# First x chunk loaded as two wide transfers, V two tiles ahead, first numerator products inside the dense tail, and another order in the last tile

## The chip, the cores and the metric

The kernel runs on one core of a Trainium2 chip. The metric is device time in microseconds (us) of that core, lower is better, given as the median of several runs. One execution was also taken with the hardware profiler: that execution has its own time, and the span inside it, from the first to the last recorded instruction, is what all the rows of the profile are measured on.

## What is computed

Two branches read the same `x` of 2048 tokens with 512 features, and a gate per token mixes them. Branch A is linear attention with 32 heads of 16 features, with a feature map made of two softmaxes; branch B is a dense layer with relu between two matrices (512 to 1376 to 512). All inputs are bf16.

```python
g = sigmoid((x * gate_w).sum(-1, keepdims=True))
# A
qkv = (x @ wqkv) split into q, k, v of 32 heads x 16
pq, pk = q @ w_phi[h], k @ w_phi[h]              # 16x16 per head
phi_q = concat([softmax(pq), softmax(-pq)], -1)  # 32 features per head
phi_k = concat([softmax(pk), softmax(-pk)], -1)
kv = einsum("bhsf,bhsd->bhfd", phi_k, v);  z = einsum("bhsf->bhf", phi_k)
num = einsum("bhqf,bhfd->bhqd", phi_q, kv)
den = einsum("bhqf,bhf->bhq", phi_q, z)[..., None] + 1e-6
a = (num / den) reshaped to (2048, 512) @ wo
# B
b = maximum(x @ w1, 0) @ w2
out = g * a + (1 - g) * b
```

The sums `kv` and `z` run over all tokens, so no output of branch A can be finished before all tokens have passed the feature map; the order of the tokens does not matter to them.

## The kernel before, in words

**Tiles.** The 2048 tokens are 16 tiles of 128 (m = 0 to 15) and four chunks of 512 (c = 0 to 3). `XT` holds x transposed, features on partitions. `PS` is the matmul memory with 8 banks of 512 f32 columns. `HT` holds the hidden layer of branch B, 11 blocks of 128 rows (kt = 0 to 10, the last with 96).

**How the order is made.** A small planner (`_Plan`, lines 14 to 55) collects instructions per engine in the order in which the program calls them, each with the names of the events that it waits for; every engine then works through its own list strictly in that order. So the order of the calls at lines 452 to 495 is the order of each engine, of the transfers that an engine issues too. The engines are TensorE (PE), VectorE (DVE), ScalarE (ACT), GpSimd (POOL) and SyncE (SP, which issues most transfers).

**Start (lines 143 to 208).** SP issues four loads of x, tokens j*128 to j*128+127 into `XS[:, j, :]` (line 145; `XS` is the first part of the tile `OT`, which is free until the end of the kernel), then four tiny loads of the gate weights into an extra column of W1. POOL issues the loads of W1 in three parts, of WV and of w_phi. Seven dummy matmuls run on PE (`warm`, line 178). Then PE transposes the first chunk of x, tile by tile, with an identity (line 186), and DVE and ACT in turn copy the four results into `XT`. SP meanwhile waits for the last part of W1 and for WV (line 163), and then issues the transposing load of Wq and Wk (`wqk`, line 164), and those of x chunks 1 to 3 (line 166). POOL waits for the last of these before it loads W2 and WO (lines 168 to 173).

**Pieces of work.**
- `hunit(c, kt)` (line 216): 4 matmuls of 512 columns for one block of the hidden layer, in banks 3, 4, 5 in turn; unit number u uses bank 3 + u % 3. ACT does the relu into `HT` (line 242). For kt = 10 the extra column gives the gate's logits: ACT copies that row (`GROW`, line 234) and issues a small transfer that lays it out by tokens in `GL` (line 238).
- `pre(half)` (line 246): Wq (half 0) or Wk (half 1) times the block-diagonal w_phi, 16 matmuls of 128 columns in banks 0, 1, 6, 7, copied out by DVE and ACT in turn (lines 263, 266). It needs `wqk`. The first of them also waits for event `cv1`, the copy of V tile 1.
- `vtile(m)` (line 315): V of a tile, 4 matmuls into bank 2 (tile 1: bank 0), copied to `VS` by DVE for the first four tiles and by ACT for the others (lines 328, 330). `VS` and `FM` have NB = 5 buffers.
- `atile(m)` (line 269): pq and pk of a tile, 8 matmuls into banks 0 and 1; then ACT takes two exponentials of 1024 columns each, of + and of - the banks (line 287). The next tile's matmuls wait for the second exponential, since they write the same banks. DVE sums and inverts (lines 290 to 299), POOL scales (lines 302 to 308), SP issues a transposing transfer of the q features to `PHQ` (line 311, event `tq`).
- `kv(m)` (line 333): 8 small matmuls that add the tile to kv and z in banks 6 and 7. `kvfin()` (line 346): four DVE instructions that mask kv and z into `KVNZ`, the last with event `kvz1`.
- `gate()` (line 360): one exponential on ACT over `GL`, and three small DVE instructions.
- `nd(m)` (line 368): numerator and denominator of a tile, 8 matmuls of 68 columns, banks 0, 1 for even m and 2, 3 for odd m; DVE inverts and multiplies (lines 380, 384, event `om`), SP issues a transposing transfer into `OT` (line 389, event `to`).
- `finB(m)` (line 392): 11 matmuls with W2 into bank 5 or 4. `finA(m)` (line 403): 4 matmuls with WO into bank 6 or 7, once `to` of the tile has landed; ACT scales by the gate (`TFA`, line 413, event `ta`). `comb(m)` (line 417): DVE adds the two halves (event `cb`), SP stores.
- `last(m)` (line 426): for tile 15 `finB` in two halves of 256 columns, with `finA` between them, and two combines and two stores.

**The order before.** 11 units of chunk 0; V tiles 0 and 1; `pre(0)`; V tile 2; `pre(1)`; V tile 3. Then for each m: `atile(m)`, `vtile(m)` from m = 4 on, one or two units of chunks 1 and 2 (22 in all: two for each of the first four tiles and in tiles 9 and 15, one otherwise), and `kv(m - 3)`. Then the 11 units of chunk 3, with the last three `kv` between them (before units 0, 2 and 6, counted from 0). Then `kvfin`, `gate`, `finB(0)`, `nd(0)`, `nd(1)`, `finB(1)`, `nd(2)`, `finA(0)`, `comb(0)`, `finA(1)`, `comb(1)`, and for m = 2 to 14 `nd(m + 1)`, `finB(m)`, `finA(m)`, `comb(m)`; then `last(15)`.

`nd(1)` and `finB(0)`, `finB(1)` wait for the relu of the very last unit (`rl{hcount[0] - 1}`).

Of the kernel before, what the change touches and what calls it, by code (L numbers as in the profile page):

```python
# [57 lines left out]
def bass_gated_mix__linear_kernel_hedgehog__dense_activation_relu__prompt_kernel(  # L58
# [31 lines left out]
    with ExitStack() as es:  # L90
# [52 lines left out]
        p.op("dve", lambda e: e.memset(WARM[:, :], 1.0), ev="warm")  # L143
        for j in range(4):
            p.dma("sp", lambda e, j=j: e.dma_start(out=XS[:, j, :], in_=x2[j * P:(j + 1) * P, :]),
                  f"x0{j}", ev=f"x0{j}")
        load_w1(0)
# [35 lines left out]
        for j in range(4):  # L183
            tp = PS[:, XB[j], :].bitcast(BF16)[:, 0:512]
            for dt in range(NDT):
                p.op("pe", lambda e, tp=tp, j=j, dt=dt: e.transpose(
                    tp[:, dt * P:(dt + 1) * P], XS[:, j, dt * P:(dt + 1) * P], IDN[:, :]),
                    after=["idn", f"x0{j}"], ev=(f"xt{j}" if dt == NDT - 1 else None))
            src = tp.rearrange("p (a b) -> p a b", a=NDT)
            dst = XT[:, :, j * P:(j + 1) * P]  # L190
            if j % 2 == 0:
                p.op("dve", lambda e, s=src, d=dst: e.tensor_copy(d, s), after=[f"xt{j}"], ev=f"xc{j}")
            else:
                p.op("act", lambda e, s=src, d=dst: e.activation(d, s, ACT.Copy), after=[f"xt{j}"], ev=f"xc{j}")
# [51 lines left out]
        def pre(half):  # L246
            PB = [0, 1, 6, 7]
            for i in range(4 * half, 4 * half + 4):
# [3 lines left out]
                after = ["wqk"] + [f"wbd{g}" for g in range(NDT)]  # L252
                if i == 0:
                    after.append("cv1")
                if i >= 4:
# [59 lines left out]
        def vtile(m):  # L315
            b = m % NB
            bank = 0 if m == 1 else 2
            prev = {0: [], 1: [], 2: ["cv0"]}.get(m, [f"cv{m - 1}"])
            for dt in range(NDT):
                p.op("pe", lambda e, m=m, dt=dt, bank=bank: e.matmul(  # L320
                    PS[:, bank, :], XT[:, dt, m * P:(m + 1) * P], WV[:, dt, :],
                    start=(dt == 0), stop=(dt == NDT - 1)),
                    after=((xready(m // 4) + ["wv"] + prev) if dt == 0 else ()),
                    ev=(f"v{m}" if dt == NDT - 1 else None))
            dst, src = VS[:, b, :, 0:64], PS[:, bank, :].rearrange("p (g c) -> p g c", g=NG)
            after = [f"v{m}"] + ([f"kv{m - NB}"] if m >= NB else [])
            if m < 4:
                p.op("dve", lambda e, d=dst, s=src: e.tensor_copy(d, s), after=after, ev=f"cv{m}")  # L328
            else:
                p.op("act", lambda e, d=dst, s=src: e.activation(d, s, ACT.Copy), after=after, ev=f"cv{m}")  # L330
# [29 lines left out]
        def gate():  # L360
# [5 lines left out]
                 after=["g"], ev="gt")  # L366

        def nd(m):
            b0 = 2 * (m % 2)
            after = [f"tq{m}", "kvz1"] + ([f"om{m - 2}"] if m >= 2 else [f"em{NT - 1}", f"cv{NT - 1}"])  # L370
            if m == 1:
                after.append(f"rl{hcount[0] - 1}")
            for g in range(NG):
# [18 lines left out]
        def finB(m):  # L392
            bank = 5 - m % 2
            after = ["w2"]
            after += [f"cb{m - 2}"] if m >= 2 else [f"rl{hcount[0] - 1}"]
            for kt in range(KT):
# [20 lines left out]
        def comb(m):  # L417
# [5 lines left out]
            p.dma("sp", lambda e, m=m, ob=ob: e.dma_start(  # L423
                out=o2[m * P:(m + 1) * P, :], in_=OSB[:, ob, :]), f"out{ob}", after=[f"cb{m}"], ev=f"out{m}")

        def last(m):
            ob = m % 3
            for hf in range(2):
                if hf == 1:
                    finA(m)  # L430
                bank = (5 - m % 2, 0)[hf]
                cs = slice(hf * 256, hf * 256 + 256)
# [7 lines left out]
            for hf in range(2):  # L440
                bank = (5 - m % 2, 0)[hf]
                cs = slice(hf * 256, hf * 256 + 256)
# [9 lines left out]
        for kt in range(KT):  # L452
            hunit(0, kt)
        vtile(0)
        vtile(1)
        pre(0)
        vtile(2)
        pre(1)
        vtile(3)
        mid = [(c, kt) for c in (1, 2) for kt in [KT - 1] + list(range(KT - 1))]  # L460
        late = [(3, kt) for kt in [KT - 1] + list(range(KT - 1))]
        done = 0
        for m in range(NT):
            atile(m)
            if m >= 4:
                vtile(m)
            want = 2 * (m + 1) if m < 4 else 8 + (m - 3) * (len(mid) - 8) // (NT - 4)
            while done < want:
                hunit(*mid[done])
                done += 1  # L470
            if m >= LAG:
                kv(m - LAG)
        cuts = {0: NT - 3, 2: NT - 2, 6: NT - 1}
        for i, u in enumerate(late):
            if i in cuts:
                kv(cuts[i])
            hunit(*u)
        kvfin()
        gate()
        finB(0)  # L480
        nd(0)
        nd(1)
        finB(1)
        nd(2)
        finA(0)
        comb(0)
        finA(1)
        comb(1)
        for m in range(2, NT - 1):
            nd(m + 1)  # L490
            finB(m)
# [57 lines left out]
```

## Time and profile before

| | |
|---|---|
| median of 3 runs | 163.28 us (163.04 to 163.32) |
| profiled execution, its own time | 162.36 us |
| span of the profiled execution | 160.1 us |
| PE / DVE / ACT / POOL busy | 149.4 / 89.0 / 78.7 / 58.2 us |
| instructions | 2385 |

By stages of the span, PE's busy time:

| stage, us from the start of the span | length | PE busy |
|---|---|---|
| until the first hidden unit, 0 to 7.25 | 7.25 | 4.37 |
| hidden units of chunk 0, to 16.90 | 9.65 | 9.65 |
| first V tiles and `pre`, to 23.40 | 6.50 | 5.48 |
| loop over 16 tiles, to 88.10 | 64.70 | 62.78 |
| hidden units of chunk 3, to 98.40 | 10.30 | 10.29 |
| first output tiles, to 111.98 | 13.58 | 11.66 |
| steady output tiles, to 150.20 | 38.22 | 38.22 |
| last tiles, to 160.10 | 9.90 | 6.93 |

How to read it: an engine's busy time counts the recorded duration of its instructions. Matmuls of 512 columns are recorded with 0.38 us each, but they overlap: back to back, four of them take 0.87 us, so one occupies PE for 0.22 us. The chain of waits follows the work back from the last instruction to what released each step. A transfer's "us to landing" counts from the start of its issue.

### The profile page before, as it was taken

The numbers are of one execution on the slowest core, as the hardware profiler recorded it, in microseconds if no ns is written. First come the engines' busy times: TensorE is split into PE (matmuls) and PEld (weight loads), VectorE is DVE, ScalarE is ACT, GpSimd is POOL, SyncE is SP. The second block draws the span as 40 slices with busy tenths as digits, with TensorE's granted clock in tenths as the row PEclk, the third lists the DMA queues.
The fourth block names the chain that finished last, engine by engine and source line by source line (L and its number), as shares of the span: only waits on it lengthen the run. The fifth ranks groups of instructions, "written<-read, shape, count | busy, mean of one in ns | idle before, by whom it ended". The sixth has DMA issues, their size and how long they took to land.

```text
span 160.1 us, 2385 instructions
## 1 busy us (share of the span) xinstructions
PE 149.4 (93%) x930; PEld 72.6 (45%) x930; DVE 89.0 (56%) x145; ACT 78.7 (49%) x116; POOL 58.2 (36%) x63
## 2 busy tenths in 40 slices
PE   6699799899999999999999998979999999999983
PEld 2444354334444444444444543534444444544442
DVE  1401391788888878687888521544455544445532
ACT  3266456877777787777777665022211111221111
POOL 7400005678888887868788800000000000000000
PEclk9999999999999999999999999999999999999999
DMA  5868994952232232332225320043222232243222
GB/s 126 259 234 186 242 185 87 359 150 66 66 70 66 66 70 66 70 68 66 66 66 70 66 66 0 0 98 92 74 68 66 70 98 66 72 92 70 66 67 64
DMA packets 41242, 15.57 MB, mean 97 GB/s; under 512 B 37584, under 2 KB 40320, under 8 KB 41232
## 3 DMA queue, kind: packets, MB, share of 16 engines
q1 hardware_dynamic: 39568, 11.54, 32.8%
q0 software_dynamic: 1088, 3.88, 7.3%
q8 instruction: 7, 0.11, 0.3%
q10 hardware_dynamic: 576, 0.01, 0.2%
q14 instruction: 3, 0.02, 0.1%
HBM read 4.41 MB, written 2.10 MB: 41 GB/s over the span
## 4 chain that ended last, share of the span: by engine, by line
PE 66%; ACT 20%; DVE 5%; DMA 3%; issue 3%; ACTq 1%; DVEq 0%
PE PS L398 19%; ACT FM L287 17%; PE PS L278 17%; PE PS L228 14%; PE PS L408 8%; DMA OT<-OTM 3%; PE PS L320 3%; PE PS L178 2%; PE PS L374 2%; ACT TFA L413 1%; DVE VS L328 1%; DVE OTM L384 1%; PE PS L340 1%; DVE WkP L263 1%; ACT GROW L234 1%
## 5 line engine op out<-in xcount | busy, mean ns | idle before, releaser
L228 PE MATMUL PS<-XT,W 128*128 128x512 bf16 (+1 forms) x176 | 41.3, 379 | 0.7 <-DVE VS L202 0.7
L398 PE MATMUL PS<-W,HT 128*128 128x512 bf16 (+1 forms) x165 | 38.1, 379 | 0.9 <-ACT EG L361 0.8
L287 ACT ACTIVATE FM<-PS 128x1024 bf16<-128x1024 f32 x32 | 31.0, 1020 | 15.7 <-PE PS L278 15.7
L302 POOL TENSOR_TENSOR FM<-FM,SC 128x1024 bf16<-128x1024 bf16 x16 | 30.9, 1929 | 12.3 <-DVE SC L293 12.3
L413 ACT ACTIVATE TFA<-PS,GT 128x512 bf16<-128x512 f32 x16 | 11.0, 687 | 46.9 <-PE PS L408 46.9
L242 ACT ACTIVATE HT<-PS 128x512 bf16<-128x512 f32 (+1 forms) x44 | 25.6, 604 | 8.1 <-PE PS L228 5.8
L290 DVE TENSOR_REDUCE ZB<-FM 128x64 f32<-128x1024 bf16 x16 | 19.5, 1220 | 14.2 <-ACT FM L287 14.2
L228 PEld LDWEIGHTS PS<-XT,W 128*128 128x128 bf16 (+1 forms) x176 | 17.3, 100 | 20.5 <-DVE VS L202 0.9
L278 PE MATMUL PS<-WqP,XT 128*128 128x512 bf16 x64 | 24.4, 381 | 2.1 <-ACT FM L287 1.3
L419 DVE SCALAR_TENSOR_TENSOR OSB<-PS,OMG,TFA 128x512 bf16<-128x512 f32 x15 | 11.3, 751 | 25.2 <-ACT TFA L413 25.2
L278 PE MATMUL PS<-WkP,XT 128*128 128x512 bf16 x64 | 24.3, 379 | 0.0
L398 PEld LDWEIGHTS PS<-W,HT 128*128 128x128 bf16 (+1 forms) x165 | 15.1, 97 | 17.4 <-issue 1.2
L295 DVE TENSOR_REDUCE ZB<-FM 128x64 f32<-128x1024 bf16 x16 | 18.6, 1161 | 0.0
L408 PE MATMUL PS<-WO,OT 128*128 128x512 bf16 x64 | 16.4, 378 | 1.5 <-DMA OT<-OTM 1.5
L308 POOL TENSOR_TENSOR FM<-FM,SC 128x512 bf16<-128x512 bf16 x16 | 16.9, 1058 | 1.3
L320 PE MATMUL PS<-WV,XT 128*128 128x512 bf16 x64 | 16.3, 379 | 0.0
L384 DVE TENSOR_TENSOR OTM<-PS,RDEN 128x512 bf16<-128x512 f32 x16 | 11.1, 691 | 0.5
L278 PEld LDWEIGHTS PS<-WqP,XT 128*128 128x128 bf16 x64 | 6.2, 97 | 11.0 <-ACT FM L287 4.5
L408 PEld LDWEIGHTS PS<-WO,OT 128*128 128x128 bf16 x64 | 5.9, 97 | 9.3 <-DMA OT<-OTM 1.7
L320 PEld LDWEIGHTS PS<-WV,XT 128*128 128x128 bf16 x64 | 6.1, 98 | 7.1
L293 DVE RECIPROCAL SC<-ZB 128x64 f32<-128x64 f32 x16 | 8.8, 553 | 0.5
L278 PEld LDWEIGHTS PS<-WkP,XT 128*128 128x128 bf16 x64 | 6.3, 98 | 5.7
(53 smaller groups left out, 89.4 us busy)
## 6 DMA issues: line engine op xcount, KB each, us to landing
out_dram<-OSB SPq DMA_DIRECT2D x15, 128.0 KB, 1.7
W<-in_B_w_dram POOLq DMA_DIRECT2D x1, 1280.0 KB, 6.6
OT<-in_A_x_dram SPq DMA_DIRECT2D x4, 128.0 KB, 2.2
W<-in_B_w_dram POOLq DMA_DIRECT2D x1, 512.0 KB, 6.2
WV<-in_A_wqkv_dram POOLq DMA_DIRECT2D x1, 512.0 KB, 7.2
WO<-in_A_wo_dram POOLq DMA_DIRECT2D x1, 512.0 KB, 6.9
W<-in_B_w_dram POOLq DMA_DIRECT2D x1, 480.0 KB, 6.7
W<-in_B_w_dram POOLq DMA_DIRECT2D x1, 384.0 KB, 4.6
```

Source lines behind the costliest of these rows:

```text
L228: p.op("pe", lambda e, c=c, kt=kt, M=M, dt=dt, bank=bank: e.matmul(PS[0:M, bank, :], W1[:, dt, kt * P:kt * P + M], XT[:, dt, c * 512:(c + ...
L242: p.op("act", lambda e, c=c, kt=kt, Mr=Mr, bank=bank: e.activation(HT[0:Mr, kt, c * 512:(c + 1) * 512], PS[0:Mr, bank, :], ACT.Relu), afte ...
L278: p.op("pe", lambda e, m=m, dt=dt, which=which, W=W: e.matmul(PS[:, which, :], XT[:, dt, m * P:(m + 1) * P], W[:, dt, :], start=(dt == 0), ...
L287: p.op("act", lambda e, o=fm5[:, :, :, s, :], i=src, s=s: e.activation(o, i, ACT.Exp, scale=(1.0 if s == 0 else -1.0)), after=[f"qk{m}"] + ...
L290: p.op("dve", lambda e, b=b: e.tensor_reduce(ZB[:, b, 64:128], FM[:, b, 1, :].rearrange("p (g f) -> p g f", f=DH), AX.X, ALU.add), after=[ ...
L295: p.op("dve", lambda e, b=b: e.tensor_reduce(ZB[:, b, 0:64], FM[:, b, 0, :].rearrange("p (g f) -> p g f", f=DH), AX.X, ALU.add), after=([f ...
L302: p.op("pool", lambda e, b=b, fk=fk: e.tensor_tensor(fk, fk, SC[:, b, 64:128].unsqueeze(2).to_broadcast([P, 2 * H, DH]), ALU.mult), after= ...
L308: p.op("pool", lambda e, b=b, fq=fq: e.tensor_tensor(fq, fq, SC[:, b, 0:32].unsqueeze(2).to_broadcast([P, H, DH]), ALU.mult), after=[f"sc{ ...
L320: p.op("pe", lambda e, m=m, dt=dt, bank=bank: e.matmul(PS[:, bank, :], XT[:, dt, m * P:(m + 1) * P], WV[:, dt, :], start=(dt == 0), stop=( ...
L384: p.op("dve", lambda e, b0=b0, r=r, ob=ob: e.tensor_tensor(OTM[:, ob, :].rearrange("p (g h d) -> p g h d", g=NG, h=HG), bass.AP(tensor=PS, ...
L398: p.op("pe", lambda e, kt=kt, M=M, m=m, bank=bank: e.matmul(PS[:, bank, :], HT[0:M, kt, m * P:(m + 1) * P], W2[0:M, kt, :], start=(kt == 0 ...
L408: p.op("pe", lambda e, t=t, m=m, bank=bank: e.matmul(PS[:, bank, :], OT[:, t, m * P:(m + 1) * P], WO[:, t, :], start=(t == 0), stop=(t == ...
```

## The change

Four things are changed; the work that is computed stays the same.

- The first 512 tokens are laid out in another way: tile j of chunk 0 now holds the tokens 4p + j for p = 0 to 127. Two loads, each of two neighbouring tokens per partition (2 KB in a row), replace the four loads. The stores of tiles 0 to 3 go to the same tokens (`orow`). The transposes of tile j wait for load j // 2.
- V runs two tiles ahead: only V tiles 0 and 1 come before the loop, behind `pre(0)` and `pre(1)` in place of ahead of them, and the loop calls `vtile(m + 2)`. All V tiles use bank 2, and ACT copies from tile 2 on. `pre(0)` no longer waits for `cv1`. Inside the loop `kv(m - 3)` comes right behind `atile(m)`, then V, then the units, which are spread otherwise: two in tiles 3, 6, 10, 13, 14 and 15, one in the others.
- In the dense tail (the 11 units of chunk 3) `kvfin` now follows `kv(15)` ahead of unit 6, `gate` stands behind unit 5, `nd(0)` ahead of unit 8 and `nd(1)` behind unit 10. `nd(0)` and all odd tiles use banks 0 and 1, the even tiles from 2 on banks 2 and 3. `nd` now runs two tiles ahead of `finB` and `finA`. The waits for the last relu become waits for the last relu of the unit's own bank (`hlast`).
- The last tile runs `finA(15)` first, then both halves of `finB`; the second half uses bank 2.

```diff
-        for j in range(4):
-            p.dma("sp", lambda e, j=j: e.dma_start(out=XS[:, j, :], in_=x2[j * P:(j + 1) * P, :]),
-                  f"x0{j}", ev=f"x0{j}")
+        xq = x2[0:512, :].rearrange("(p j) d -> p j d", j=4)
+        oq = o2[0:512, :].rearrange("(p j) d -> p j d", j=4)
+        def orow(m):
+            return oq[:, m, :] if m < 4 else o2[m * P:(m + 1) * P, :]
+        for i in range(2):
+            p.dma("sp", lambda e, i=i: e.dma_start(out=XS[:, 2 * i:2 * i + 2, :], in_=xq[:, 2 * i:2 * i + 2, :]),
+                  f"x0{i}", ev=f"x0{i}")
...
-                    after=["idn", f"x0{j}"], ev=(f"xt{j}" if dt == NDT - 1 else None))
+                    after=["idn", f"x0{j // 2}"], ev=(f"xt{j}" if dt == NDT - 1 else None))
...
-                if i == 0:
-                    after.append("cv1")
...
-            bank = 0 if m == 1 else 2
-            prev = {0: [], 1: [], 2: ["cv0"]}.get(m, [f"cv{m - 1}"])
+            bank = 2
+            prev = [f"cv{m - 1}"] if m else []
...
-            if m < 4:
+            if m < 2:
...
+        def hlast(bank):
+            return f"rl{[u for u in range(hcount[0]) if 3 + u % NH == bank][-1]}"
         def nd(m):
-            b0 = 2 * (m % 2)
-            after = [f"tq{m}", "kvz1"] + ([f"om{m - 2}"] if m >= 2 else [f"em{NT - 1}", f"cv{NT - 1}"])
-            if m == 1:
-                after.append(f"rl{hcount[0] - 1}")
+            b0 = 0 if m == 0 or m % 2 else 2
+            after = [f"tq{m}", "kvz1"]
+            if m == 0:
+                after.append(f"em{NT - 1}")
+            elif m == 2:
+                after += [f"cv{NT - 1}", hlast(3)]
+            else:
+                after.append(f"om{max(m - 2, 0)}")
...
-            after += [f"cb{m - 2}"] if m >= 2 else [f"rl{hcount[0] - 1}"]
+            after += [f"cb{m - 2}"] if m >= 2 else [hlast(bank)]
...
-                out=o2[m * P:(m + 1) * P, :], in_=OSB[:, ob, :]), f"out{ob}", after=[f"cb{m}"], ev=f"out{m}")
+                out=orow(m), in_=OSB[:, ob, :]), f"out{ob}", after=[f"cb{m}"], ev=f"out{m}")
...
+            finA(m)
             for hf in range(2):
-                if hf == 1:
-                    finA(m)
-                bank = (5 - m % 2, 0)[hf]
+                bank = (5 - m % 2, 2)[hf]
...
+        pre(0)
         vtile(0)
+        pre(1)
         vtile(1)
-        pre(0)
-        vtile(2)
-        pre(1)
-        vtile(3)
...
             atile(m)
-            if m >= 4:
-                vtile(m)
-            want = 2 * (m + 1) if m < 4 else 8 + (m - 3) * (len(mid) - 8) // (NT - 4)
-            while done < want:
+            if m >= LAG:
+                kv(m - LAG)
+            if m + 2 < NT:
+                vtile(m + 2)
+            while done < (min(m + 1, 14) * (len(mid) - 4)) // 14 + 2 * max(m - 13, 0):
                 hunit(*mid[done])
                 done += 1
-            if m >= LAG:
-                kv(m - LAG)
-        cuts = {0: NT - 3, 2: NT - 2, 6: NT - 1}
         for i, u in enumerate(late):
-            if i in cuts:
-                kv(cuts[i])
+            if i == 0:
+                kv(NT - 3)
+            if i == 2:
+                kv(NT - 2)
+            if i == 6:
+                kv(NT - 1)
+                kvfin()
+            if i == 8:
+                nd(0)
             hunit(*u)
-        kvfin()
-        gate()
+            if i == 10:
+                nd(1)
+            if i == 5:
+                gate()
         finB(0)
-        nd(0)
-        nd(1)
-        finB(1)
         nd(2)
         finA(0)
         comb(0)
-        finA(1)
-        comb(1)
-        for m in range(2, NT - 1):
-            nd(m + 1)
+        for m in range(1, NT - 1):
+            if m + 2 < NT:
+                nd(m + 2)
             finB(m)
             finA(m)
             comb(m)
```

More of the change, by code (lines that the diff above doesn't have):

```diff
@@ L440, in last @@
             for hf in range(2):
-                bank = (5 - m % 2, 0)[hf]
+                bank = (5 - m % 2, 2)[hf]
                 cs = slice(hf * 256, hf * 256 + 256)
```

## The prediction

> **What bounds the kernel now.** I read the chain of waits by engine first, then windows by stage, then the chain in order of time and the timelines around the places that the change touches.
>
> ```profile
> PE 66%; ACT 20%; DVE 5%; DMA 3%; issue 3%; ACTq 1%; DVEq 0%
> ```
>
> A third of the chain is not PE's. ACT's 20% lie in one place, the loop over tiles; the rest are joints between stages. The windows tell the stages apart (after the length comes PE's busy time).
>
> ```profile
> 23.40:88.10 64.70, 62.78 (x374) 29.73 (x375) 49.47 (x62) 48.21 (x68) 49.85 (x48) 1.00 0.39 94
> 88.10:98.40 10.30, 10.29 (x69) 4.81 (x65) 3.30 (x8) 6.94 (x13) 3.61 (x4) 1.00 0.23 51
> 98.40:111.98 13.58, 11.66 (x86) 5.81 (x87) 6.11 (x13) 2.29 (x5) 0.00 (x0) 1.00 0.23 54
> 111.98:146.95 34.97, 34.97 (x232) 17.11 (x230) 17.05 (x30) 6.88 (x11) 0.00 (x0) 1.00 0.30 74
> ```
>
> The dense tail (88.10 to 98.40) and the steady output tiles have no hole; the first output tiles have 1.92 of holes. Windows from one `atile` to the next, for tiles 6, 7 and 8, 9, 10 and 11:
>
> ```profile
> 47.14:51.07 3.93, 3.87 (x25) 1.86 (x25) 3.21 (x5) 2.92 (x5) 3.20 (x4) 1.00 0.30 67
> 51.07:59.07 8.00, 7.74 (x48) 3.83 (x48) 6.40 (x9) 6.41 (x10) 6.47 (x7) 1.00 0.32 68
> 59.07:63.81 4.74, 4.74 (x29) 2.31 (x30) 4.02 (x5) 3.72 (x7) 3.85 (x4) 1.00 0.25 56
> 63.81:67.57 3.76, 3.70 (x25) 1.76 (x23) 2.40 (x5) 2.60 (x5) 3.03 (x4) 1.00 0.34 74
> 67.57:71.59 4.02, 3.87 (x25) 1.88 (x26) 3.29 (x5) 3.01 (x5) 2.71 (x3) 1.00 0.30 67
> ```
>
> A tile with V and one unit takes 3.93: its own matmuls, then both exponentials, under which PE does the rest. Tiles 7 and 8 have a gate row on ACT between them and take 0.14 over twice that. Tile 9, with two units, is PE's: 4.74 without a hole; the next, whose matmuls follow at once, takes 3.76, and the one after that 4.02.
>
> **The start.** Two of four loads of x go. In PE's timeline the fourth is late:
>
> ```profile
> 1.46 3.17 PE L178 MATMUL PS<-WARM 128*128 128x512 bf16 x7 [1.46 <-DVE WARM L143]
> 4.42 1.02 PE L186 MATMUL PS<-IDN,OT 128*128 128x128 bf16 x12
> 6.12 0.40 PE L186 MATMUL PS<-IDN,OT 128*128 128x128 bf16 x4 [0.68 <-DMA OT<-in_A_x_dram]
> ```
>
> and in the chain the first units and what follows them stand so:
>
> ```profile
> 7.25 9.66 PE PS L228 x44
> 16.91 1.74 PE PS L320 x8
> ...
> 19.51 1.05 PE PS L258 x16
> ...
> 23.41 1.91 PE PS L278 x8
> ```
>
> The second wide load is issued second, not fourth; I take it to land before 5.4, so that four more transposes follow the twelve (which end at 5.44) at their pace of some 0.09 and end near 5.8 in place of 6.52. The first unit came 0.73 after that and would come at 6.54: 0.71 sooner (bounds: 0 if the load still lands at 6.1; no loss, since the same 512 KB are issued sooner). The 44 matmuls then end at 16.2.
>
> Next on PE now stands `pre(0)`; before, 1.74 of V tiles stood ahead of it. It needs `wqk`, which SP issues once WV and W1 are in; the change does not move these. SP's timeline, and the page's row of issues with the time to landing:
>
> ```profile
> 11.49 4.17 SPq L164 DMA_TRANSPOSE PHQ<-in_A_wqkv_dram  x1
> ```
>
> ```profile
> PHQ<-in_A_wqkv_dram SPq DMA_TRANSPOSE x1, 6.5
> ```
>
> 11.49 + 6.5 = 17.99. So the 0.71 ends in a wait: PE is idle for 1.8, `pre(0)` starts at 18.05, and the wide loads are worth nothing (0.71 if that wait were gone). From 19.51 to 23.41 the order was `pre(0)`, V, `pre(1)`, V with DVE's copies between them, and is the same now, with other V tiles: 3.90. `atile(0)` starts at 21.95, **1.46 sooner**. What goes is the removed `cv1` wait and the two V tiles ahead. Bounds: `wqk` was surely there at 19.51 (then 0), and PE could not begin before 16.2 (then 3.3); I take the issue-to-landing row. The four gate-weight loads move up 0.9 us on SP; nobody needs them before kt = 10.
>
> **The loop.** V moves two tiles into it, 0.87 of PE each, and kv goes to the front of the free time.
>
> ```profile
> 63.56 0.25 PE PS L340 x8
> ```
>
> One unit (9.66 / 11 = 0.87 to 0.88), V and kv are 1.98, beside 3.93 - 1.91 = 2.02 that a tile leaves: hidden, as in tiles 4 to 8, which had that content already. kv first in the queue costs nothing: the scaled features of tile m - 3 are done more than a tile earlier. ACT gets two copies more, 0.5 each, within the 2 us that it has per tile. Two units with V come in tiles 3, 6, 10 and 13. Sum: tiles 0, 2, 9 at 3.93 = 11.79; tile 1 4.07 (behind the first gate row); three groups of 4.74 + 3.76 + 4.02 = 37.56; tile 13 4.74; tile 14 without V 3.76; tile 15 1.91 + 1.73 + 0.25 = 3.89. Together 65.81, where before had 88.10 - 23.41 = 64.69: **1.12 more**. (PE's work alone would be 62.3, but the exponentials exclude that; I allow 0.5 to either side.) The loop ends at 87.76.
>
> **The dense tail.** It had no hole, so `nd(0)` and `nd(1)` add 0.26 each (row below). But `gate` now stands ahead of `kvfin` on DVE, and so ahead of `nd(0)`. ACT's, PE's and DVE's timelines of before:
>
> ```profile
> 93.86 0.60 ACT L242 ACTIVATE HT<-PS 128x512 bf16<-128x512 f32 x1 [0.27 <-PE PS L228]
> ...
> 98.92 0.21 ACT L361 ACTIVATE EG<-GL 128x16 f32<-128x16 f32 x1
> ```
>
> ```profile
> 93.91 4.48 PE L228 MATMUL PS<-XT,W 128*128 128x512 bf16 x20
> ```
>
> ```profile
> 94.11 0.42 DVE L349 TENSOR_TENSOR KVNZ<-PS,M 128x256 bf16<-128x256 f32 x1 [3.56 <-PE PS L340]
> ...
> 94.87 0.17 DVE L353 SCALAR_TENSOR_TENSOR KVNZ<-PS,M 128x16 bf16<-128x16 f32 x1
> 99.16 0.17 DVE L363 TENSOR_SCALAR EG<-EG 128x16 f32<-128x16 f32 x1 [4.12 <-ACT EG L361]
> ...
> 99.65 0.17 DVE L365 TENSOR_SCALAR OMG<-GT 128x16 f32<-128x16 f32 x1
> ```
>
> On before's clock: unit 5's relu ends at 94.46 and the gate's exponential follows; DVE's three start 99.16 - 98.92 = 0.24 behind it and take 99.82 - 99.16 = 0.66, to 95.36; then `kvfin` with 95.04 - 94.11 = 0.93, done at 96.3. Overlap of neighbours on one engine may take 0.1 off. PE, two units past `kv(15)`, is at `nd(0)` at 93.91 + 1.73 = 95.64. It waits some 0.5 (0 if ACT were free far sooner, 0.65 at most by these rows), and units 8 to 10 wait behind it on PE. `nd(1)` comes three units later (2.6), when DVE has emptied `nd(0)`'s bank (two instructions). The exponential itself waits for the logits of chunk 3, whose transfer ACT issues behind unit 0, some 4 us ahead of it:
>
> ```profile
> GL<-GROW ACTq DMA_DIRECT2D x4, 2.0 KB, 2.6
> ```
>
> That hides it; were it later, the relus queued behind the exponential on ACT would be late too, and PE through its banks. On SP `nd(0)`'s transfer queues behind tile 15's q features only, which POOL has released by then. The tail is 10.30 + 0.52 + 0.5 = 11.32, **1.02 more**, and ends at 99.08.
>
> **The output tiles.** The chain before:
>
> ```profile
> 99.17 2.54 PE PS L398 x11
> ...
> 105.72 1.04 PE PS L408 x4
> ...
> 111.73 0.26 PE PS L374 x8
> ```
>
> The last relu held `finB(0)` from 98.40 to 99.17, and `finA(0)` had to wait for the first transposed tile until 105.72. Both waits go: bank 5's last relu is two units old, and `nd(0)`, `nd(1)` run ahead of `finB(0)`: tile 0's transfer starts some 3 us sooner than PE needs it. What is late next is only PE: 34.97 / 10 = 3.497 a tile in the window above. After: 15 tiles less one `nd` = 52.20, `finA(15)` 0.87 (four matmuls, as V), two halves of `finB(15)` 2.40 (11 x 0.109 each, half of a 512-column matmul), 0.16 until the last is out: 99.08 + 55.63 = 154.71. The last rows of PE and DVE:
>
> ```profile
> 156.18 1.36 PE L436 MATMUL PS<-W,HT 128*128 128x256 bf16 x11
> 157.15 0.91 DVE L443 SCALAR_TENSOR_TENSOR OSB<-PS,OMG,TFA 128x256 bf16<-128x256 f32 x2 [1.90 <-ACT TFA L413]
> ```
>
> Before, PE's last ended at 156.18 + 1.36 = 157.54, 2.56 before the span's end; now a half combine (0.46), 0.02, and the 2.04 from the end of the combines (158.06) to 160.1: 2.52. `finA(15)`'s scaling is done under the halves, and with `nd` two tiles ahead its transfer has long landed. This stage takes 58.15 in place of 61.70: **3.55 less**. Stores with a stride in tiles 0 to 3 are free: nobody waits for them for three tiles.
>
> **Sum.** -1.46 + 1.12 + 1.02 - 3.55 = -2.87. The profiled execution's 162.36 becomes 159.5 (span 157.2); the median of the runs is 0.92 above that execution, and the same difference takes 163.28 to **160.4**.
>
> **Rivals.**
> - *The gate does not hold `nd(0)`* (ACT gets to its exponential sooner, or PE is later there): 0.5 less, 159.9. Against it stands only the order on DVE.
> - *`wqk` lands late.* The trace only shows that it was there at 19.51. Then the start gains nothing: 160.4 + 1.46 = 161.9. For it: PE never waited for it, so its landing is untested.
> - *The wide loads free the transfers.* WV, and with it `wqk`, comes sooner; at most `pre(0)` starts at 16.2: 158.6. Against it: the same bytes move.
> - *PE falls to half rate in the hole ahead of `pre(0)`*, the slower side. There are two rates: 3.17 / 7 = 0.45 a matmul from 1.46 on, 9.66 / 44 = 0.22 from 7.25 on (the granted clock reads 1.00 in both). If the 1.8 us hole brings the slow rate back, PE's 3.48 us of `pre` and V double (the stage has 0.42 to spare: +3.06) and `atile(0)`'s 1.74 too: 160.4 + 4.8 = 165.2. It decides from 7.2 us of half rate on (half of that, less 0.42, is 3.2). At the start it lasted from 1.46 to at most 7.25, 5.8 us, which is too little; and the hole of 0.86 ahead of 19.51 (V ends at 18.65) left no trace. [...]
> - *Late `wqk` and a longer loop together* eat it all: no change, 163.2.
>
> **How the numbers follow.** Forecast 0.52, gate hidden 0.18, late `wqk` 0.15, early transfers 0.05, half rate 0.05, nothing left 0.05. Range 159.3 to 162.0: the loop's 0.5 below the gate case, and the late `wqk` above; the other three cases, 0.15, lie outside. 0.2% is 0.33 us, about what a measurement of this kernel can tell from no change: faster 0.90, same 0.05, slower 0.05.
>
> **What would show it.** Right: first unit near 6.5; PE idle ahead of `pre(0)` until about 18.0, released by the transfer of Wq and Wk; `atile(0)` at 21.95; tiles of 3.93 but for four of 4.74; `nd(0)` waiting 0.5 on DVE; no idle of PE from `finB(0)` on. Wrong: `pre(0)` at 19 or later, one-unit tiles over 4.0, a half-rate stretch, `finA(0)` waiting for a transfer.

## The result, and the profile after

The changed kernel takes 158.82 us (median of 4 runs, 158.37 to 159.26) beside 163.3 for the kernel before (4 runs, 163.04 to 163.38): a ratio of 0.9728, 95% interval 0.9699 to 0.9758, 4.5 us less. The forecast was 160.4 with a range from 159.3 to 162.0: the direction was right, the size 1.6 short. The ratios here and below leave out runs that are over 1.5% above the quickest of their kernel, so a ratio can look a little better than the medians beside it. The profiled execution of the changed kernel takes 158.37, with a span of 156.5 (before 162.36 and 160.1).

The chain of waits at the start of the changed kernel (start, length, what):

```profile
4.17 6.84 DMA WV<-in_A_wqkv_dram
...
11.09 6.49 DMA PHQ<-in_A_wqkv_dram
17.57 0.05 issue
17.62 1.07 PE PS L262 x16
...
21.53 1.91 PE PS L282 x8
```

The start is now a chain of transfers, as forecast: WV, then the transposing load of Wq and Wk, then `pre(0)`. It is 0.4 sooner than forecast (11.09, 17.62 and 21.53 in place of 11.49, 18.05 and 21.95). PE's timeline shows what became of the wide loads:

```profile
4.42 1.46 PE L192 MATMUL PS<-IDN,OT 128*128 128x128 bf16 x16
7.22 9.66 PE L234 MATMUL PS<-XT,W 128*128 128x512 bf16 x43 [1.34 <-DMA W<-in_B_w_dram]
```

All 16 transposes run through, as assumed, but the first unit starts at 7.22 and not 6.54: it now waits for the first part of W1. The page's rows of issues, before and after, with the time to landing last:

```profile
W<-in_B_w_dram POOLq DMA_DIRECT2D x1, 384.0 KB, 4.6
```

```profile
W<-in_B_w_dram POOLq DMA_DIRECT2D x1, 384.0 KB, 5.8
```

What x gained, W1 lost: the transposes end at 5.88 in place of 6.52, and the first part of W1, which POOL issues while SP issues x, takes 5.8 to landing in place of 4.6. This is no matter of one execution: in all five traces with narrow loads this row reads 4.6 to 4.9, in all thirteen with wide loads 5.0 to 6.6.

Windows of the changed kernel (length, then PE's busy time): `pre` and V, the loop with `kv(12)`, the dense tail, the output tiles.

```profile
17.62:21.53 3.91, 3.63 (x39) 2.48 (x41) 3.23 (x6) 2.65 (x5) 0.00 (x0) 1.00 1.45 182
21.53:87.30 65.77, 63.88 (x378) 29.54 (x386) 48.85 (x62) 49.14 (x69) 49.19 (x48) 1.00 0.43 97
87.30:98.45 11.15, 10.60 (x75) 5.21 (x76) 5.47 (x13) 7.39 (x15) 4.21 (x4) 1.00 0.26 57
98.45:156.50 58.05, 55.14 (x357) 27.84 (x361) 26.75 (x47) 11.38 (x17) 0.00 (x0) 1.00 0.30 71
```

Forecast were 3.90, 65.81, 11.32 and 58.15. The loop, tile 2 to tile 6, in windows from one `atile` to the next:

```profile
29.54:33.48 3.94, 3.58 (x16) 1.50 (x17) 3.21 (x5) 2.92 (x5) 3.17 (x4) 1.00 1.07 359
33.48:38.21 4.73, 4.73 (x29) 2.31 (x30) 4.00 (x5) 3.72 (x6) 3.92 (x5) 1.00 0.26 57
38.21:41.97 3.76, 3.65 (x24) 1.62 (x23) 2.40 (x5) 2.63 (x5) 3.02 (x4) 1.00 0.31 70
41.97:45.90 3.93, 3.88 (x24) 1.73 (x25) 3.20 (x5) 2.92 (x5) 2.64 (x3) 1.00 0.46 71
45.90:50.64 4.74, 4.68 (x28) 2.31 (x30) 4.01 (x5) 3.73 (x6) 3.92 (x5) 1.00 0.25 55
```

Tiles 3 and 6, with two units, are PE's at 4.7; the one behind takes 3.76. In the dense tail the gate stands ahead of `kvfin` on DVE, and `nd(0)` waits for it (DVE's timeline, then PE's):

```profile
93.55 0.17 DVE L367 TENSOR_SCALAR EG<-EG 128x16 f32<-128x16 f32 x1 [3.19 <-ACT EG L365]
...
94.04 0.17 DVE L369 TENSOR_SCALAR OMG<-GT 128x16 f32<-128x16 f32 x1
94.13 0.42 DVE L353 TENSOR_TENSOR KVNZ<-PS,M 128x256 bf16<-128x256 f32 x1
...
94.88 0.17 DVE L357 SCALAR_TENSOR_TENSOR KVNZ<-PS,M 128x16 bf16<-128x16 f32 x1
```

```profile
92.61 0.41 PE L344 MATMUL PS<-VS,FM 128*128 128x65 bf16 x8
92.86 1.89 PE L234 MATMUL PS<-XT,W 128*128 128x512 bf16 x8
95.19 0.42 PE L385 MATMUL PS<-KVNZ,PHQ 128*128 128x68 bf16 x8 [0.44 <-DVE KVNZ L357]
```

`kv(15)` ended at 93.02, but `kvfin` starts at 94.13, behind the gate's third instruction. The chain from there is PE's alone:

```profile
98.45 2.38 PE PS L409 x11
100.83 0.26 PE PS L385 x8
101.08 0.86 PE PS L419 x4
...
149.78 1.73 PE PS L419 x8
151.50 2.42 PE PS L446 x22
```

No `finA` waits for a transfer, and both halves of the last `finB` follow at once.

### The profile page after: what moved, and what is told of

It is laid out like the page before. It is cut to its first block, busy times and chain, and to the rows that moved or that the text cites. A ratio compares the mean times of both kernels' runs of the same rounds, so it can differ in the third digit from the quotient of the medians.

```text
span 156.5 us, 2370 instructions
## 1 busy us (share of the span) xinstructions
PE 147.3 (94%) x913; PEld 71.8 (46%) x930; DVE 87.7 (56%) x143; ACT 79.5 (51%) x118; POOL 58.2 (37%) x63
## 3 DMA queue, kind: packets, MB, share of 16 engines
q1 hardware_dynamic: 39536, 11.54, 34.8%
## 4 chain that ended last, share of the span: by engine, by line
PE 68%; ACT 15%; DMA 9%; DVE 2%; issue 2%; POOL 2%; ACTq 0%; POOLq 0%; SPq 0%
PE PS L409 23%; PE PS L282 18%; ACT FM L291 14%; PE PS L234 10%; PE PS L419 9%; DMA WV<-in_A_wqkv_dram 4%; DMA PHQ<-in_A_wqkv_dram 4%; PE PS L324 3%; PE PS L385 3%; PE PS L446 2%; POOL W L140 2%; PE PS L344 1%; DVE WkP L267 1%; PE PS L262 1%; DVE VS L332 0%
## 5 line engine op out<-in xcount | busy, mean ns | idle before, releaser
L234 PE MATMUL PS<-XT,W 128*128 128x512 bf16 (+1 forms) x166 | 40.3, 379 | 1.9 <-DMA W<-in_B_w_dram 1.3
L395 DVE TENSOR_TENSOR OTM<-PS,RDEN 128x512 bf16<-128x512 f32 x16 | 11.1, 691 | 0.6
L334 ACT ACTIVATE VS<-PS 128x512 bf16<-128x512 f32 x14 | 8.4, 603 | 0.0
```

Of the source, the lines that this page charges most:

```text
L234: p.op("pe", lambda e, c=c, kt=kt, M=M, dt=dt, bank=bank: e.matmul(PS[0:M, bank, :], W1[:, dt, kt * P:kt * P + M], XT[:, dt, c * 512:(c + ...
```

## Theories

Theory of the stages: the change is worth what the two traces show, term by term, and what the median moved beyond that (4.5 against 3.6 of span) comes from the start, which is not the same in every execution. Rival: some part of the change carries a gain of its own that the two traces do not show, the wide loads first of all, since they are the part that was priced at nothing.

For each experiment one execution was traced. The columns: issue of the load of Wq and Wk, start of `pre(0)`, start of the first `atile`, and the time from there to the end of PE's last matmul, all us of the trace.

| kernel | Wq, Wk issued | `pre(0)` | first `atile` | from there to PE's end |
|---|---|---|---|---|
| before | 11.49 | 19.51 | 23.41 | 134.13 |
| e7, before and dummies | 11.27 | 19.50 | 23.40 | 134.13 |
| e1, before and wide loads | 12.10 | 21.51 | 25.41 | 134.05 |
| e3, new tail alone | 11.68 | 19.57 | 23.46 | 131.60 |
| e4, new start and loop alone | 11.47 | 18.43 | 22.61 | 134.93 |
| changed kernel | 11.09 | 17.62 | 21.53 | 132.38 |
| e5, the same | 12.07 | 18.94 | 23.12 | 132.35 |
| e14, the same | 11.49 | 17.80 | 21.71 | 132.38 |
| e2, changed, narrow loads | 11.54 | 17.93 | 21.84 | 132.40 |
| e13, the same as e2 | 11.19 | 18.50 | 22.69 | 132.37 |
| e6, changed and dummies | 12.19 | 18.62 | 22.53 | 132.37 |
| e12, changed, short warm-up | 11.46 | 18.45 | 22.63 | 132.35 |
| e8, changed, gate late | 11.80 | 18.34 | 22.25 | 131.78 |
| e9, changed, Wq and Wk early | 9.82 | 16.98 | 21.16 | 132.36 |
| e10, e8 and e9 | 8.53 | 16.45 | 20.63 | 131.75 |
| e11, changed, V tile 0 first | 12.41 | 18.82 | 22.00 | 132.36 |
| e15, e8, e9 and e11 | 9.26 | 17.49 | 21.03 | 131.77 |
| e16, e8 and e11 | 11.79 | 18.13 | 21.39 | 131.77 |

The end is taken from the row of the last matmuls, in the changed kernel 151.34 + 2.57 = 153.91:

```profile
151.34 2.57 PE L446 MATMUL PS<-W,HT 128*128 128x256 bf16 x22
```

The last column is the main reading of this study: it is 132.35 to 132.40 in all nine traces that have the changed kernel's order from the first `atile` on, whatever the start did (and 131.75 to 131.78 in the four with the gate late). All that varies up to PE's end lies ahead of the first `atile`, and there by up to 1.6 us for one and the same kernel (21.53, 23.12, 21.71).

## The experiments

**e1, wide loads alone.** The kernel before with the two wide loads and `orow`:

```diff
-        for j in range(4):
-            p.dma("sp", ... out=XS[:, j, :], in_=x2[j * P:(j + 1) * P, :]) ...
+        for i in range(2):
+            p.dma("sp", ... out=XS[:, 2 * i:2 * i + 2, :], in_=xq[:, 2 * i:2 * i + 2, :]) ...
```

> The kernel before with nothing but the two wide loads of x (tiles 0 to 3 hold tokens 4p + j, their stores go to the same tokens). Theory A: the first hidden unit then waits for the first part of W1, which lands at about 7.1 us, so it starts at 7.2 as before; WV lands some 0.4 sooner, but pre(0) still stands behind V tiles 0 and 1 and the copy of V tile 1, so nothing of that reaches the end: 0 against before (163.3, within 0.3). Rival B: the wide loads carry the gain that was not forecast: the first unit or pre(0) starts 0.7 to 1.6 us sooner and the whole is 0.7 to 1.6 shorter.

162.92 beside 162.64 (23 runs of before): ratio 1.0000, 0.9954 to 1.0045. Theory A holds. The traced execution was a long one (164.24, span 162.1) and shows one way in which runs differ, in PE's timeline:

```profile
7.76 11.14 PE L234 MATMUL PS<-XT,W 128*128 128x512 bf16 x43 [1.43 <-DMA W<-in_B_w_dram]
```

The first part of W1 came later still (6.4 to landing), and the 44 unit matmuls took 11.14 in place of 9.66: the first eight of them start 0.43 apart, the half rate of the warm-up, the later ones 0.22.

**e2, narrow loads in the changed kernel** (the edit of e1 the other way round).

> The changed kernel with the four narrow loads of x put back, all else as changed. Theory A: the load of Wq and Wk is issued when WV is in; with narrow loads WV lands near 11.4 in place of 11.0, the load is issued near 11.49 in place of 11.09, pre(0) starts at about 18.0 in place of 17.62 and the first attention tile at 21.95 in place of 21.53: 0.4 longer than the changed kernel, 159.2. Rival B: the time at which WV lands differs from run to run by as much, whatever the loads of x: no difference, 158.8, or issue times of Wq and Wk that scatter about 11.3 in both.

158.83 beside 162.64: 0.9763 (0.9715 to 0.9810), against 158.82 of the changed kernel. Rival B holds: no difference. Its trace has the load at 11.54 and the first `atile` at 21.84, as forecast for narrow loads, but that is no cause yet; e13 and e14 settle it.

**e3, the new tail, output order and last tile alone** (`nd`, `hlast`, `finB`, `last` and the calls from the dense tail on, in the kernel before).

> The kernel before with the new dense tail, the new output order and the new last tile alone; start and loop as before. Theory A: the stages add up as the two traces show them: tail 0.85 longer, output tiles 3.65 shorter, so 2.8 less than before: 160.5 at a median of 163.3. Rival B: the 0.9 us by which the median moved more than the profiled span sit in the output stage: 3.7 less, 159.6. If the part alone gives 2.8 in time but the spans of the runs of before are longer than 160.1, the profiled execution of before was a quick one.

159.66 beside 162.64: 0.9809 (0.9758 to 0.9860), 3.0 less in the medians. From the first `atile` on the trace saves 134.13 - 131.60 = 2.53. Theory A is the nearer one; 0.3 more lie outside the span (below). Its last clause was right too: the spans of the runs of before, measured beside it, go from 160.1 to over 162.

**e4, the new start and loop alone** (the changed kernel with the old tail, output order and last tile).

> The changed kernel with the old tail, output order and last tile: wide loads, V two tiles ahead and the new loop alone. Theory A: first attention tile 1.88 sooner, loop 1.08 longer: 0.8 less than before, 162.5. Rival B: what the median moved beyond the profiled span sits here: 1.7 less, 161.6.

161.82 beside 162.64: 0.9910 (0.9875 to 0.9945), 0.8 less, as Theory A has it (both theories were worked out from 163.28, and before is 0.64 lower on this chip, so the differences count and not the times). From the first `atile` on it is 0.80 longer, so its start saves 1.6. This trace too caught a half-rate start (44 matmuls in 11.52), and `atile` still came 0.8 sooner than in the trace of before. e3 and e4 together make 3.8, e5 measures 3.9: the parts add up, and no part holds a gain beyond its stage but for the 0.1 to 0.3 outside the span (below).

**e5, the changed kernel again**, beside 16 runs of before.

> The changed kernel once more, beside many runs of before. Theory A: PE's half rate at the start lasts longer in some runs than in others (in the profiles so far the first units took 9.66 us, or 11.1 to 11.5 with matmuls of 631 ns). Before pays all of that, the changed kernel pays it less the 0.74 that it waits for Wq and Wk anyhow. So its runs spread over about 1 us where before spreads over 2, its quickest stands 3.7 to 3.9 under the quickest of before, and its median 4 or more under the median of before where the chip starts slow often. Rival B: the gain is one number, 4.4, in quick and slow runs alike.

159.03 beside 162.94: 0.9737 (0.9688 to 0.9785). Its runs go from 158.65 to 159.95, those of before from 162.35 to 165.10; the quickest are 3.7 apart, the medians 3.9. That fits Theory A, although the medians moved less than 4 and six runs say little of a spread. The traced execution was the longest of its six, and here the granted clock (the number ahead of the transfers' share) shows one cause, beside the late W1:

```profile
5.35:7.00 1.65, 0.00 (x1) 1.00 0.68 164
7.00:7.20 0.20, 0.00 (x0) 1.00 0.81 287
7.20:7.40 0.20, 0.00 (x0) 1.00 0.70 270
7.40:7.60 0.20, 0.00 (x0) 0.93 0.82 294
7.60:7.80 0.20, 0.00 (x0) 0.50 0.98 322
7.80:8.00 0.20, 0.03 (x1) 0.50 1.25 486
8.00:10.90 2.90, 2.90 (x7) 0.50 0.88 348
10.90:11.00 0.10, 0.10 (x2) 0.57 0.35 133
11.00:11.20 0.20, 0.20 (x3) 1.00 0.31 123
```

PE has nothing to do from 5.35 until W1's first part lands at 7.97; at 7.57 its clock is halved, for 3.4 us.

**e6, dummies against the idle time.** In the changed kernel:

```diff
+        warm(5)          # behind the 16 transposes of x
```

> The changed kernel with five dummy matmuls (as in the warm-up, into the unused bank 7) on PE between the transposes of x and the first unit, where it idles for 1.3 us. Theory A: an idle PE there lets the half rate go on into the first units; kept busy, it runs at full rate from the first unit on in nearly all runs: quickest time as that of the changed kernel (within 0.2), the upper half of its runs up to 1 us quicker, spread under 0.4. Rival B: the spread comes from elsewhere (transfers): no change in median and spread. Rival C: the dummies delay the first unit when the rate is low: median up to 0.9 longer.

159.54 beside 162.94: 0.9749 (0.9689 to 0.9808), runs from 158.36 to 160.78. Theory A falls: neither median nor spread became smaller. Rival C is not excluded: the median is 0.5 above that of e5, with intervals that overlap. The longest run has a granted clock of 0.989 over its span, so a stretch of half rate came in spite of the dummies. The trace has the units at full rate, and is late all the same:

```profile
7.21 9.66 PE L235 MATMUL PS<-XT,W 128*128 128x512 bf16 x43
18.62 1.07 PE L263 MATMUL PS<-Wbd,PHQ 128*128 128x128 bf16 x16 [1.76 <-DMA PHQ<-in_A_wqkv_dram]
```

So there is a second source of spread, the landing of WV (at 12.10 here, at 11.01 in the first trace), behind which Wq and Wk are loaded (issued at 12.19 here).

**e7, dummies in the kernel before** (`warm(3)` at the same place).

> The kernel before with three such dummy matmuls behind the transposes, where PE idles for 0.7. Theory A: the slow starts go: median down to its quickest runs, about 0.3 to 0.9 less, spread under 0.5. Rival B: the spread is not PE's rate: median and spread as before.

162.83 beside 162.94: 0.9983 (0.9945 to 1.0022), runs from 162.28 to 164.44. Theory A falls here too: the dummies do not remove the long runs. None of the long runs of before was traced; what their records of the clock say stands further below.

**e8, the gate behind `nd(1)`.**

```diff
             if i == 10:
                 nd(1)
-            if i == 5:
                 gate()
```

> The changed kernel with gate() moved behind nd(1), so that its three DVE instructions no longer stand ahead of kvfin; the computation is the same. Theory A (the wait of 0.44 of nd(0) on DVE is on the path): 0.45 less than the changed kernel on the same chip, and the output stage follows at once. Rival B: hidden, no difference.

158.83, 0.9728 (0.9683 to 0.9772): in time not to be told from e5. In the trace the stage behind the first `atile` is 0.60 shorter (131.78 in place of 132.38), and PE's timeline shows `nd(0)` without a wait, 1.97 behind the start of `kv(15)` in place of 2.58:

```profile
93.33 0.41 PE L344 MATMUL PS<-VS,FM 128*128 128x65 bf16 x8
93.58 1.89 PE L234 MATMUL PS<-XT,W 128*128 128x512 bf16 x8
95.30 0.42 PE L385 MATMUL PS<-KVNZ,PHQ 128*128 128x68 bf16 x8
```

**e9, Wq and Wk loaded sooner.**

```diff
-        p.wait("sp", ["w12", "wv"])
+        p.wait("sp", ["w11"])
```

> The changed kernel with SP's wait ahead of the load of Wq and Wk changed from the last part of W1 and WV to the second part of W1 (which lands near 9); nothing else depends on that wait. Theory A (the landing of Wq and Wk, and so that of WV, sets the first attention tile): the load is issued near 9, lands near 16, pre(0) follows the 44 unit matmuls at once (16.9 in place of 17.6 to 18.9) and the first attention tile starts at 20.8 in place of 21.5 to 23.1: 0.7 to 1.5 less, about 157.8. Rival B: the transposing load then holds up the last part of W1 and WV, the units wait for it, and nothing is won, or up to 2 lost.

158.79 beside 162.46: 0.9743 (0.9683 to 0.9803), runs from 157.81 to 161.66. The trace is Theory A's: issued at 9.82, `pre(0)` right behind the units, first `atile` at 21.16. The time alone does not show a gain, since half of the runs are long, and for those Rival B is not excluded.

**e10, e8 and e9 together.**

> e9 and e8 together: gate() behind nd(1), and the earlier load of Wq and Wk. Theory A: the two add up, since they lie in different stages: 0.6 less than e9 from the first attention tile to the end (131.78 in place of 132.38 from its start to PE's last matmul), about 157.2 in time. Rival B: not additive, as e9.

157.10 beside 162.46: 0.9646 (0.9590 to 0.9702). That is the quickest median found, ahead of both kernels, although two of the six runs are long (159.99 and 161.52). The changed kernel was not run on this chip; the interval lies below that of e14 (from 0.9737 on) and overlaps that of e5 (from 0.9688 on) by 0.0014. Theory A: both terms are in its trace, 20.63 and 131.75.

**e11, V tile 0 ahead of `pre(0)`.**

```diff
-        pre(0)
         vtile(0)
+        pre(0)
         pre(1)
```

> The changed kernel with V tile 0 ahead of pre(0), where PE waits for Wq and Wk, and pre(1) right behind pre(0). Theory A: the wait is on the path, but behind it DVE's and ACT's eight copies of pre set the pace, 2.6 for four on DVE, so that the first attention tile comes 3.4 to 3.6 behind pre(0) in place of 3.90: 0.3 to 0.5 less. Rival B: PE sets the pace there, V tile 0 fills the hole and 0.87 go.

157.96 beside 162.46: 0.9722 (0.9673 to 0.9772), all six runs lie below the changed kernel's usual 159. The step is larger than Theory A said and smaller than Rival B said: 22.00 - 18.82 = 3.18 from `pre(0)` to `atile` in place of 3.91, although Wq and Wk came later than in any other run (issued at 12.41):

```profile
16.98 1.03 PE L324 MATMUL PS<-WV,XT 128*128 128x512 bf16 x4
18.82 2.40 PE L262 MATMUL PS<-Wbd,PHQ 128*128 128x128 bf16 x32 [0.82 <-DMA PHQ<-in_A_wqkv_dram]
```

So 0.73 of the 0.87 go. In the chain of this trace DVE's first copy (`WqP`, 0.70 from 19.26) still holds PE's matmuls of `pre` until 20.01: the mechanism of Theory A is there, but it holds back less than was said.

**e12, a short warm-up** (`warm(3)` in place of `warm(7)`).

> The changed kernel with three dummy matmuls at the start in place of seven, so that PE is idle for longer and more units run at half rate. Theory A: the 44 unit matmuls take 11.1 or more in place of 9.66 in nearly all runs; of that the changed kernel's wait for Wq and Wk takes up some 0.7 to 1.8, so the whole is 0.3 to 1.5 longer. Rival B: half rate at the start is not on the path of the changed kernel: no difference.

159.89 beside 162.46: 0.9829 (0.9775 to 0.9883), 0.6 to 1.1 longer than the changed kernel's three medians, which are from other chips. Theory A: the half rate is on the path, and the wait for Wq and Wk takes up part of it.

```profile
6.38 12.23 PE L234 MATMUL PS<-XT,W 128*128 128x512 bf16 x43 [0.85 <-DVE M L203]
18.45 1.06 PE L262 MATMUL PS<-Wbd,PHQ 128*128 128x128 bf16 x16
```

The units start 0.84 sooner than in the changed kernel, take 2.57 longer, and `pre(0)` comes 0.83 later.

**e13 and e14, narrow and wide on one chip.**

> The changed kernel with four narrow loads again, now on the same chip as e14. Theory A (after the runs so far: WV landed between 11.1 and 12.2 with wide loads, between 11.3 and 11.7 with narrow ones): the wide loads are worth nothing, both medians within 0.3 of each other. Rival B: wide loads bring the first attention tile 0.3 to 0.4 sooner, as the two profiles in hand would have it: e14 0.3 to 0.4 quicker.

> The changed kernel, as the other half of e13. Its trace from the first attention tile to PE's last matmul takes 132.4 whatever the start did (Theory A: all that varies lies before the first attention tile); Rival B: other stages vary too, by 0.3 or more.

Beside 162.47: narrow 158.75, 0.9748 (0.9709 to 0.9788); wide 159.29, 0.9778 (0.9737 to 0.9818). The wide loads bring nothing that these runs can show; the medians stand 0.5 apart, more than the 0.3 of Theory A and the other way round, and the intervals overlap. Over all traces with the old wait Wq and Wk were issued between 11.09 and 12.41 with wide loads, and between 11.19 and 11.68 with narrow ones; if anything, the wide loads make that later. Rival B falls, and e14's last column is Theory A's.

**e15 and e16, more of them together.**

> The changed kernel with gate() behind nd(1), V tile 0 ahead of pre(0), and Wq and Wk loaded behind the second part of W1. Theory A: V tile 0 takes DVE's copy out of the middle of pre's, 0.7 less from pre(0) to the first attention tile (3.2 in place of 3.9), but with Wq and Wk early it puts 0.87 of PE ahead of pre(0): about even with e10, 157.0, quick runs near 156.8. Rival B: the two add up: 156.4.

> The changed kernel with gate() behind nd(1) and V tile 0 ahead of pre(0), the wait for WV and W1 as it was. Theory A: 0.6 (gate) and 0.7 to 0.9 (V tile 0) less than the changed kernel: 157.4, and it depends less on how the start runs than e10. Rival B: one of the two is hidden behind the other: 158.

e15: 157.43, 0.9658 (0.9614 to 0.9701), level with e10 as Theory A has it, but 0.4 over its number, and the step from `pre(0)` to `atile` is 3.54 in its trace and not 3.2. e16: 157.80, 0.9717 (0.9666 to 0.9768), in time nearer to Rival B's 158 than to Theory A's 157.4. Its trace has both terms all the same (3.26 from `pre(0)` to `atile`, 131.77); that the rest is its start is argued, not shown.

## Why the prediction was wrong

Step by step, against the changed kernel's trace:

- **Start.** The mechanism was right: the load of Wq and Wk takes the place of V and `cv1`, and the wide loads are worth nothing (e1, e13, e14). One step in it was wrong: the first unit came at 7.22 and not at 6.54, since W1's first part landed later, so PE waited 0.74 for Wq and Wk and not 1.8. Both end in the same wait, so the sum did not feel it. The first `atile` at 21.95 was forecast; 21.53 and 21.71 were traced, and 23.12 where PE ran at half rate. The 0.4 by which the first trace beats the forecast is one execution's start, not the change: luck.
- **Loop.** 65.81 forecast, 65.77 measured; the pattern of 3.93, 4.74 and 3.76 came as priced.
- **Dense tail.** 11.32 forecast, 11.15 measured. The gate's hold on `nd(0)` was there; e8 prices it at 0.6 (forecast 0.5).
- **Output tiles.** 58.15 forecast, 58.05 measured, no wait left.
- **Outside the span.** Taken as 2.26 for both; the changed kernel has 1.87 in its profiled execution and 1.86 to 1.98 in its three other first runs, but 1.94 to 2.16 in the twelve runs of e5 and e14, where runs of before have 2.13 to 2.23. With the new tail alone (e3) it is 1.81 to 1.87, with the new start and loop alone (e4) 1.91 to 2.14. So both parts shorten it, and the two do not add up. The traces do not show why; that stays open.
- **The step that failed** is the last one of the sum, "the median of the runs is 0.92 above that execution, and the same difference takes 163.28 to 160.4". It took the 0.92 for a fixed distance that both kernels have. It is not fixed: in the five sets of runs the median of before lies 0.94, 0.28, 0.58, 0.10 and 0.11 above its traced execution, and in three sets that of the changed kernel 0.45, 0.66 and 0.92 above its own. Of 61 further runs of before 37 lie between 162.1 and 162.9, 8 between 163.0 and 163.5, and 16 from 164.1 up; the traced execution was of the first group, the three runs of the median of the second. So 0.5 of the 1.6 are this distance (0.92 against 0.45), 0.4 the sooner start of the one trace, 0.4 what lies outside the span, 0.3 small terms of the three stages, all of the same sign. It is the largest of four terms of like size: without it the forecast would have been 159.9, still 1.1 over.

That the distance is smaller for the changed kernel holds for the first set alone; in the two later ones it is larger than that of before. What is shown is that a bad start costs the changed order less. A start that costs PE 1.5 to 1.9 (the units in 11.1 to 11.5) moves the first `atile` of the old order by 2.0 (e1, with W1 0.5 later), but that of the changed order by 0.8 to 1.6 (22.61 in e4, 22.69 in e13, 23.12 in e5, against 21.53 to 21.84): the wait for Wq and Wk takes up part of it.

How many of the long runs have such a start can be read in part from the record, which gives each run's granted clock as a mean over its span. Half rate for 3.4 of 162 us makes 0.989. Six of the sixteen runs of before from 164.1 up read 0.988 to 0.990, and the other 55 runs all read 0.998 or more. Of the experiments' own runs twelve read below 0.995, in eleven sets, and each is the longest of its set (in e10 the two longest). So a stretch of half rate is behind those. For the other ten long runs of before it stays open: a mean of 1.000 does not exclude it, as the traced run of e1 shows (164.24, with half rate up to 10.8 by the starts of its units). It also stays open why the dummies of e6 and e7 did not remove the long runs, what sets the middle group of before apart, and why W1's first part lands up to 1.6 and WV up to 1.3 apart from one execution to the next.

The rival of a half rate was put at the wrong place: not in the hole ahead of `pre(0)`, but at the first unit (halved at 7.57 in e5, ahead of its start at 7.97, and at 7.61 in e13, behind its start at 7.32), and in runs of before too, by the clocks just named. What a hole of 1.8 does to PE's rate no trace had shown when the forecast was made. Two traces show it now for this place: behind 1.76 in e6 and 1.45 in e8 the 16 matmuls of `pre(0)` take 1.07, beside 1.05 in before. Beside before's 162.47 on the chip of e14 the changed kernel is 3.2 less, on the others 3.9 and 4.5: the forecast of 2.9 lies near the lower of these.

Two more points on the rivals. The one of sooner transfers named 158.6, next to the measured 158.82, but its mechanism is not what happened: WV was 0.4 sooner in the first trace and no sooner in e5, e14 and e1. And late `wqk` with a longer loop would not have eaten it all: their own terms, 1.46 and 0.5, give 162.4 and not 163.2.

## What to carry to other kernels

Before a difference worked out in one trace is applied to a median, look where the runs of one kernel differ: here everything from the first attention tile to PE's last matmul repeats within 0.05 us and what lies ahead of it does not, so a change that puts a wait into the start also changes what a bad start costs. Price a sooner transfer together with the ones beside it: the wide loads brought x in sooner and W1's first part 1.2 later, so that the first unit began no sooner (7.22 beside 7.25 in the first two traces). When small work (`gate`) is moved forward, read who stands behind it on its engine: 0.6 us went to three instructions ahead of `kvfin`.

## What the runs showed of the hardware

PE's clock was halved at 7.57 in e5 after 2.2 us of idle, and in e13 at 7.61 although PE had worked in between (idle from 5.15 to 6.19 and from 6.59 to 7.32, 1.8 in all); both times for 3.4 us. Not long before, the transposes from 4.29 and 4.32 on had run at the quick rate: 16 took 1.06 in e5, 12 took 0.83 in e13, where 16 took 1.91 in e1. Windows of e13 (the clock is the number ahead of the transfers' share):

```profile
7.00:7.50 0.50, 0.18 (x1) 1.00 1.04 402
7.50:8.00 0.50, 0.50 (x3) 0.61 1.13 374
8.00:10.00 2.00, 2.00 (x6) 0.50 1.04 405
10.00:11.00 1.00, 1.00 (x4) 0.50 0.40 152
11.00:12.00 1.00, 1.00 (x6) 0.99 0.00 0
```

No rule for the idle time follows: in e11 PE idled for 1.79 us (5.69 to 7.48), and the units behind it ran at full rate (9.66); in e6 dummies filled the idle time, and its units took 9.66 too.

In e1, e4 and e12 the first matmuls of the units ran at half rate (the units took 11.14, 11.52 and 12.23 in place of 9.66) while the column of the granted clock reads 1.00 in every window from 7 to 12. The same holds for the warm-up of before and of the changed kernel's first trace: 3.17 for seven matmuls, 0.45 each, at 1.00 in the column. The page of the changed kernel's trace has no row of the clock at all, and in its windows the column reads 1.00 throughout. So an early 1.00 in that column proves nothing (the prediction took it for a reading in the warm-up); the durations tell the rate.

A single transfer of 512 KB (WV), issued at 4.16 or 4.17, landed between 11.01 us (the first trace of the changed kernel) and 12.33 (e11).
